# Who loads what first: moving the opening transfers between two queues, and new first orders, in a fused attention and gMLP kernel

## The chip, the cores and the metric

The kernel runs on one core of one Trainium2 chip. The metric is device microseconds for one execution, median of several runs. The engines are TensorE (PE in the profile, with its weight loads as PEld), VectorE (DVE), ScalarE (ACT), GpSimd (POOL) and SyncE (SP), which here only issues transfers. SP and ScalarE each have a queue of transfers of their own (q1 and q10 in the profile), and the transfers of both run on the same 16 DMA engines.

## The reference

The computation is a block of linear attention followed by a gMLP mixer, both with a layer norm in front and a residual behind, on x of 2048 rows by 512 columns in bfloat16:

```python
def _A_ref(x, wqkv, wo):                       # 32 heads of 16
    q, k, v = split(x @ wqkv)
    phi = lambda t: jnp.where(t > 0, t + 1, jnp.exp(t)) + 1e-06
    pq, pk = (phi(q), phi(k))
    kv = jnp.einsum('bhsd,bhse->bhde', pk, v)
    z = jnp.einsum('bhsd->bhd', pk)
    num = jnp.einsum('bhqd,bhde->bhqe', pq, kv)
    den = jnp.einsum('bhqd,bhd->bhq', pq, z)[..., None] + 1e-06
    return merge(num / den) @ wo

h  = x + _A_ref(_layernorm(x), wqkv, wo)
z  = gelu(_layernorm(h) @ w_in)                # 1792 columns, two halves of 896
g  = w_sp @ _layernorm(z[:, 896:]) + b_sp[:, None]
h2 = h + (z[:, :896] * g) @ w_out
```

Only the first step matters for the change: the layer norm of x, and the projection of its rows by the 512 columns of `wqkv` that make the keys.

## The kernel before

x is cut into 16 tiles of 128 rows. For each tile VectorE takes the statistics of the rows (`BNStats`, L576), joins them into mean and variance (the aggregate, L580), and later normalises the tile (L611) once one over the root of the variance is there. For tiles 0 to 3 ScalarE makes that root as an exponential of a logarithm (L590, L592); for later tiles GpSimd does it in pairs (L595, L597). The normalised tile must be transposed before TensorE can project it. Tiles 0 to 3 are transposed on TensorE itself, four products with the identity (L645), and ScalarE copies the result out of PSUM (L652); tiles 4 to 15 are transposed by SP's transfers (`DMA_TRANSPOSE`, L637), one after the other.

TensorE projects a tile to keys with four products of 128x512 (L734), ScalarE and VectorE turn the projections of a pair of tiles into `phi(k)` (L711, L713, L714, L717, L720), and TensorE adds up `xn^T phi(k)` over all tiles (L766). Query projections (L748) come for groups of four tiles. The later stages are the per-head products, the output projection with the residual (L904), the gMLP input (L936, L967), the mixing over rows (L1006) and the last projection (L1024).

Before there is anything to do, TensorE runs idle products on constants (L564, `keep_busy`): eight of 128x512 from the start (`WARM = 8`), two more behind the first tile's statistics, one behind its root, and four halves of 128x256 behind the transposes of tiles 0 and 1. Nobody reads their results.

Nothing is scheduled by the chip. Every operation is registered with `op(...)` in the order of the program's text and numbered; the list `ORDER` gives the order in which all of them are issued, and each engine runs its own in that order. `SLOT` gives each tile of PSUM (banks 0 to 7) and of the other pools its place. Waits are worked out from the data: an operation waits by semaphore for what it reads, and for the earlier users of its place. A wait at the head of an engine's list holds all that stands behind it on that engine. Both lists were found by a search outside this program.

The transfers at the start are registered at L510 and after. Before the change they are: on SP x tile 0, tile 2, tile 3, the query weights (512 columns of `wqkv`), tiles 4 and 5 in one transfer, then 6 and 7, 8 and 9, 10 and 11, 12 to 15; on ScalarE x tile 1 and the key weights, and behind these two the load of ScalarE's table (L555). A tile of x is 128 KB, the key weights and the query weights are 512 KB each. The value weights and what follows are loaded by GpSimd much later.

`g.first_of["act"]` is a list of operations that everything registered later on ScalarE must follow.

Of the kernel before, what the change touches and what calls it, by code (L numbers as in the profile page):

```python
# [12 lines left out]


ORDER = [
# [34 lines left out]
]  # L50
SLOT = [
# [104 lines left out]
class Program:  # L156
# [14 lines left out]
    def op(self, eng, cost, fn, r=(), w=(), bias=0.0, after=(), dma=None, nbytes=0, land=2.0, lag=None,  # L171
           mode=0):
        o = Op()
        o.eng, o.fn, o.cost, o.seq = eng, fn, cost, len(self.ops)
        o.bias, o.land, lag = bias + self.bias, land, self.LAG[eng] if lag is None else lag
        o.late, o.start, o.mode = self.late, None, mode
        o.after, o.deps, o.tiles = list(after) + self.first_of.get(eng, []), {}, []
        o.marked, o.sem, o.semval, o.grp, o.bytes, o.lag = False, None, None, dma, nbytes, lag
        o.raw = set()
        for x in list(r) + list(w):  # L180
            t = getattr(x, "tile", None)
            if t is not None and t not in o.tiles:
                o.tiles.append(t)
                t.ops.append(o)
        rk = [k for x in r for k in x.keys]
        wk = [k for x in w for k in x.keys]
        for k in rk:
            p = self.writer.get(k)
            if p is not None:
                o.deps[p] = True  # L190
                o.raw.add(p)
        for k in wk:
            p = self.writer.get(k)
            if p is not None:
                o.deps[p] = True
            for q in self.readers.get(k, ()):
                if q is not o:
                    o.deps[q] = True
        for k in rk:
            self.readers.setdefault(k, []).append(o)  # L200
        for k in wk:
            self.writer[k] = o
            self.readers[k] = []
        self.ops.append(o)
        return o
# [149 lines left out]
def bass_sequential_preLN__linear_attn_block__mixer_gmlp__prompt_kernel(  # L355
# [11 lines left out]
    _, S, D = A_x.shape  # L367
# [5 lines left out]
    TPG = GW // P  # L373
    NP = NT // 2
    assert D == 512 and KD == 4 and NG == 4 and FH == KF * P and 512 < FH <= 1024
    WARM = 8
    EPS_PHI, EPS_DEN, EPS_LN = 1e-6, 1e-6, 1e-5
    CG = 32
# [30 lines left out]
    wqkv = View(s_w3, 0, [KD, 3 * D], BF16)  # L409
# [65 lines left out]
    def bank(i):  # L475
        return lambda a: a[:, i, :]
# [4 lines left out]
    g = Program(nc)  # L481
# [12 lines left out]
    def load(eng, name, dst, src, nbytes, bias=0.0, behind=(), cost=0.5):  # L494
        o = op(eng, cost, lambda e: e.dma_start(dst.ap(), src), w=[dst], dma=(name, False), nbytes=nbytes,
               bias=bias, land=2.3)
        for p in behind:
            o.deps[p] = True
        return o

    w3 = A_wqkv.rearrange("(c p) f -> p c f", p=P)
# [3 lines left out]
    def load_x(eng, a, b, bias=BIG, **kw):  # L505
        more = {2: 40e3, 3: 60e3, 4: 70e3}.get(a, 0)
        xl[a] = load(eng, f"x{a}", x[a:b, :], x_dram[a * P:b * P, :].rearrange("(n p) d -> p n d", p=P),
                     int((b - a) * P * D * 2 + more), bias, **kw)

    load_x("sp", 0, 1)  # L510
    load_x("act", 1, 2)
    load("act", "wk", wqkv[:, D:2 * D], w3[:, :, D:2 * D], D * D * 2)
    load_x("sp", 2, 3)
    load_x("sp", 3, 4)
    load("sp", "wq", wqkv[:, 0:D], w3[:, :, 0:D], D * D * 2)
    for a in (4, 6):
        load_x("sp", a, a + 2)
    for a in (8, 10):
        load_x("sp", a, a + 2)
    load_x("sp", 12, 16)  # L520
# [39 lines left out]
    warm = []  # L560

    def keep_busy(n, cost, after, behind=()):
        row = nc.const_aps.tensor(1.0, (P, n), BF16)
        o = op("pe", cost, lambda e: e.matmul(idle(bank(0)).ap()[:, 0:n], lhsT=row[:, 0:P], rhs=row, start=True,  # L564
                                                 stop=True), w=[idle()], bias=BIG, after=after)
        for p in behind:
            o.deps[p] = True
        return o

    for i in range(WARM):  # L570
        warm = [keep_busy(512, MM, warm)]


    def stats(src, st):
# [381 lines left out]
    for tg in range(NG):  # L956
        g.bias = -GROUP * tg - 40.0
        for f0 in range(0, KF, 2):
# [18 lines left out]
         behind=[last_T[hT[0].store]])  # L977

    def load_wsp(tg, after):
        for st in range(NT):  # L980
            dst = wsp[tg][st, :]
            o = op("sp", 1.3, lambda e, dst=dst, st=st: e.dma_start_transpose(
                dst.ap(), B_w_sp[tg * GW:(tg + 1) * GW, st * P:(st + 1) * P]),
               w=[dst], dma=(f"wsp{tg}", True), nbytes=P * GW * 2, land=2.7, bias=-120.0 - 20 * tg, after=after)
            after = [o]
        return after

    bsp = Tile(BS)
    behind = [last_T[xT[0].store]]
    for tg in range(NG):  # L990
        g.late = tg > 0
        behind = load_wsp(tg, behind + ([last_T[hT[0].store]] if tg == 1 else []))
# [91 lines left out]
```

## Time and profile before

| | us |
|---|---|
| median of 3 runs | 241.08 (240.99 to 241.31) |
| the profiled execution | 241.31 |
| its span, first to last instruction | 240.1 |
| TensorE busy in the span | 235.3 |
| VectorE busy | 132.8 |
| ScalarE busy | 78.6 |
| first statistics on VectorE start | 3.50 |
| first key projection starts | 7.05 |
| third key projection starts | 9.61 |

Times in the views are microseconds from the start of the span. In a timeline row the first number is the start, the second how long, then the engine, the line of the kernel and the operation; what stands in square brackets is how long the engine was idle before and what it waited for. A queue's own instructions carry a q (SPq, ACTq). In a row of transfers the last number is the time from issue to landing. TensorE's products overlap: one is listed with its whole way through the array, so the distance from start to start is what a product costs.

### The profile page before, as it was taken

How to read it: one execution, taken by the hardware profiler on the slowest of the kernel's cores; microseconds unless marked ns; L12 is line 12 of the kernel's file. 1: busy time of each engine (PE TensorE's matmuls, PEld its weight loads, DVE VectorE, ACT ScalarE, POOL GpSimd, SP SyncE). 2: the span in 40 equal slices, each digit the busy share in tenths (PEclk: the TensorE clock that was granted, in tenths of full speed). 3: DMA queues.
4: the chain of work that ended last, by engine and by line, in shares of the span. 5: the costliest groups of instructions: out<-in, count | busy, mean ns of one | idle time of the engine just before them, and what ended most of it. 6: DMA issues, size and time to landing. Idle time of an engine off the chain costs nothing.

```text
span 240.1 us, 3026 instructions
## 1 busy us (share of the span) xinstructions
PE 235.3 (98%) x1172; PEld 110.2 (46%) x1194; DVE 132.8 (55%) x269; ACT 78.6 (33%) x101; POOL 33.3 (14%) x84
## 2 busy tenths in 40 slices
PE   7999999999999999999999999999999999999996
PEld 2544444554444444444444444444444444444443
DVE  4898884489999882938533233351332523323444
ACT  3783843884487698665400000000000000000000
POOL 7131303000334514235000000000000000000000
DMA  6930539950214463369444444445500200000022
GB/s 215 310 77 19 105 70 252 322 104 3 44 33 93 122 83 66 67 172 159 108 91 107 90 104 94 109 93 88 148 24 0 67 24 0 0 3 0 0 87 88
DMA packets 56702, 21.83 MB, mean 91 GB/s; under 512 B 50704, under 2 KB 55824, under 8 KB 56688
## 3 DMA queue, kind: packets, MB, share of 16 engines
q1 hardware_dynamic: 54928, 16.62, 33.3%
q0 software_dynamic: 944, 4.33, 5.4%
q10 hardware_dynamic: 816, 0.70, 0.9%
q8 instruction: 9, 0.15, 0.3%
q14 instruction: 5, 0.04, 0.1%
HBM read 7.47 MB, written 2.10 MB: 40 GB/s over the span
## 4 chain that ended last, share of the span: by engine, by line
PE 96%; DMA 1%; DVE 1%; issue 1%
PE ps L1006 40%; PE ps L936 10%; PE ps L1024 10%; PE ps L967 10%; PE ps L766 6%; PE ps L904 6%; PE ps L734 6%; PE ps L748 6%; DMA xh<-in_A_x_dram 1%; DVE small L576 1%; PE ps L645 1%; PE ps L858 0%; PE ps L838 0%; PE ps L782 0%; PE ps L874 0%
## 5 line engine op out<-in xcount | busy, mean ns | idle before, releaser
L1006 PE MATMUL ps<-wsp,pk_xn_z 128*128 128x512 bf16 x328 | 72.9, 379 | 0.4
L1013 DVE TENSOR_TENSOR e<-ps,e 128x512 bf16<-128x512 f32 x28 | 19.4, 692 | 66.1 <-PE ps L1006 66.1
L1006 PEld LDWEIGHTS ps<-wsp,pk_xn_z 128*128 128x128 bf16 x336 | 32.9, 98 | 39.6
L936 PE MATMUL ps<-win,hT 128*128 128x512 bf16 (+1 forms) x127 | 26.1, 352 | 0.1
L967 PE MATMUL ps<-hT,win 128*128 128x512 bf16 x108 | 25.8, 379 | 0.2
L1024 PE MATMUL ps<-wout,xT_pq_z 128*128 128x512 bf16 (+2 forms) x118 | 24.6, 366 | 0.1
L1006 PE MATMUL ps<-wqkv_wsp,pk_xn_z 128*128 128x512 bf16 x110 | 24.2, 379 | 0.1
L945 DVE BATCH_NORM_STATS2 small<-pk_xn_z 128x6 f32<-128x512 bf16 (+1 forms) x32 | 18.2, 606 | 10.6 <-ACT pk_xn_z L941 10.6
L576 DVE BATCH_NORM_STATS2 small<-xh 128x6 f32<-128x512 bf16 x32 | 21.0, 675 | 3.5 <-DMA xh<-in_A_x_dram 3.5
L711 ACT ACTIVATE e<-ps 128x1024 bf16<-128x1024 f32 x16 | 16.4, 1029 | 11.5 <-PE ps L734 8.1
L936 PEld LDWEIGHTS ps<-win,hT 128*128 128x128 bf16 x128 | 12.5, 98 | 12.7
L972 ACT ACTIVATE xT_pq_z<-ps 128x1024 bf16<-128x1024 f32 (+1 forms) x16 | 14.2, 915 | 10.0 <-PE ps L967 10.0
L1024 PEld LDWEIGHTS ps<-wout,xT_pq_z 128*128 128x128 bf16 x119 | 11.5, 98 | 13.0
L1030 DVE TENSOR_TENSOR e<-ps,xh 128x512 bf16<-128x512 f32 (+2 forms) x17 | 11.2, 660 | 11.3 <-PE ps L1024 11.3
L1006 PEld LDWEIGHTS ps<-wqkv_wsp,pk_xn_z 128*128 128x128 bf16 x112 | 11.0, 98 | 13.2
L967 PEld LDWEIGHTS ps<-hT,win 128*128 128x128 bf16 x112 | 10.9, 98 | 12.5 <-DVE xh L909 0.2
L941 ACT ACTIVATE pk_xn_z<-ps 128x896 bf16<-128x896 f32 x16 | 14.5, 918 | 4.6 <-PE ps L936 4.6
L597 POOL TENSOR_TENSOR small<-small 128x2 f32<-128x2 f32 x22 | 15.8, 720 | 1.3
L766 PE MATMUL ps<-pk_xn_z 128*128 128x512 bf16 x64 | 15.9, 379 | 0.0
L734 PE MATMUL ps<-wqkv_wsp,xT_pq_z 128*128 128x512 bf16 x63 | 15.6, 379 | 0.1
L748 PE MATMUL ps<-xT_pq_z,wqkv_wsp 128*128 128x512 bf16 x60 | 14.6, 379 | 0.3 <-issue 0.2
L904 PE MATMUL ps<-pk_xn_z,xT_pq_z 128*128 128x512 bf16 x63 | 14.2, 379 | 0.2 <-issue 0.2
(71 smaller groups left out, 173.0 us busy)
## 6 DMA issues: line engine op xcount, KB each, us to landing
out_dram<-e SPq DMA_DIRECT2D x15, 128.0 KB, 1.7
win<-in_B_w_in_dram POOLq DMA_DIRECT2D x1, 1792.0 KB, 11.3
xh<-in_A_x_dram SPq DMA_DIRECT2D x4, 256.0 KB, 6.2
wout<-in_B_w_out_dram POOLq DMA_DIRECT2D x1, 896.0 KB, 6.8
wsp<-in_B_w_sp_dram SPq DMA_TRANSPOSE x48, 2.7
wqkv_wsp<-in_A_wqkv_dram ACTq DMA_DIRECT2D x1, 512.0 KB, 4.4
wqkv_wsp<-in_A_wqkv_dram SPq DMA_DIRECT2D x1, 512.0 KB, 5.6
xh<-in_A_x_dram SPq DMA_DIRECT2D x1, 512.0 KB, 7.4
```

Source lines behind the costliest of these rows:

```text
L576: op("dve", dve_c(512), lambda e: e.bn_stats(s6.ap(), src.ap()), r=[src], w=[s6])
L711: op("act", act_c(n), lambda e: e.activation(lo.ap(), t(flat).ap(), ACT.Exp), r=[t()], w=[lo])
L734: i = e.matmul(t(bank(ti)).ap(), lhsT=lhs.ap()[:, c, :], rhs=rhs.ap()[:, c, :], start=(c == 0), stop=(c == KD - 1))
L748: r_ = e.matmul(t(bank(i)).ap(), lhsT=lhs.ap()[:, c, :], rhs=rhs.ap()[:, c, :], start=(c == 0), stop=(c == KD - 1))
L766: r = e.matmul(txk[h](bank(i)).ap(), lhsT=xx.ap()[:, c * P:(c + 1) * P], rhs=kk.ap(), start=(n == 0), stop=(n == NT - 1))
L904: i = e.matmul(t(bank(ti)).ap(), lhsT=l.ap()[:, c, :], rhs=mw[c, :].ap(), start=(c == 0), stop=(c == KD - 1))
L936: k = e.matmul(t(bank(i)).ap()[:, 0:b - a], lhsT=l.ap()[:, c, :], rhs=win[c, a:b].ap(), start=(c == 0), stop=(c == KD - 1))
L945: op("dve", dve_c(b - a), lambda e, s6=s6, src=src: e.bn_stats(s6.ap(), src.ap()), r=[src], w=[s6])
L967: k = e.matmul(t(bank(i)).ap(), lhsT=l.ap()[:, c, :], rhs=r_.ap()[:, c, :], start=(c == 0), stop=(c == KD - 1))
L1006: k = e.matmul(t(bank(0)).ap(), lhsT=l.ap()[:, s - a, :], rhs=r_.ap()[:, s - a, :], start=(s == 0), stop=(s == NT - 1))
L1013: op("dve", dve_c(512), lambda e: e.tensor_tensor(gb().ap(), t(bank(0)).ap(), bsp().ap()[:, tg * GW:(tg + 1) * GW], ALU.add), r=[t(), bsp( ...
L1024: k = e.matmul(t(bank(0)).ap()[:, 0:b - a], lhsT=l.ap()[:, fc, :], rhs=wout[fc, a:b].ap(), start=(fc == 0), stop=(fc == KF - 1))
```

## The change

The key weights stay on ScalarE, but ScalarE's table load now stands first in its list, and the weights' transfer waits for the end of the first idle product on TensorE. x tile 1 goes from ScalarE's queue to SP's, so that SP issues tiles 0, 1, 2, 3, then 4 and 5, then the query weights, then the rest. The number `GATE` says behind which idle product the weights wait.

The first part of `ORDER`, up to where the first stage ends, is replaced by another order of the same operations, and the places in PSUM of that part are dealt out anew. What this does to the first instructions of each engine:

- VectorE before: statistics 0, aggregate 0, statistics 1, aggregate 1, normalise 0, statistics 2, normalise 1, aggregate 2, statistics 3, normalise 2, aggregate 3, normalise 3, then statistics of 4 and 5. After: statistics 0 and 1, aggregates 0 and 1, statistics 2, normalise 0, aggregate 2, normalise 1 and 2, statistics 3, aggregate 3, statistics 4, normalise 3.
- ScalarE before: root 0, root 1, copy of transpose 0, root 2, copy 1, root 3, copies 2 and 3. After: roots 0, 1, 2, copies 0 and 1, root 3, copies 2 and 3.
- TensorE before: ten idle products, transposes 0, an idle product and two halves, transposes 1, key projection 0, transposes 2, key projection 1, a half, transposes 3, a half, key projections 2 and 3. After: eleven idle products, transposes 0, two halves, transposes 1, two halves, transposes 2, key projections 0 and 1, transposes 3, key projections 2 and 3. Both go on with the sixteen products of the first query projection, then six (before) or four (after) products of L766, then key projections 4 and 5.
- GpSimd: the constants are made in another order; the identity comes after the selection matrix.

All line numbers behind the new lines grow by one to three: the key projection is L734 before and L737 after. The work is the same.

```diff
 ORDER = [
-    0, 3, 4, 5, 6, 27, 1, 2, 13, 24, 14, 28, 29, 30, 31, 32, 33, 15, 21, 16, 7, 8, 34, 35, 123, 124, 11, 12, 22, 18,
...
+    0, 1, 17, 12, 23, 24, 13, 20, 10, 21, 16, 22, 11, 35, 42, 36, 43, 2, 3, 49, 26, 28, 29, 30, 31, 32, 33, 34, 25, 27,
...
 SLOT = [
-    0, 1, 1, 2, 1, 4, 0, 4, 0, 2, 1, 2, 1, 6, 1, 2, 0, 6, 0, 2, 2, 6, 0, 6, 0, 2, 6, 0, 6, 6, 2, 6, 2, 0, 6, 1, 6, 6,
...
+    0, 1, 2, 3, 3, 0, 0, 2, 0, 4, 1, 4, 1, 6, 1, 4, 0, 6, 0, 4, 0, 6, 0, 6, 2, 2, 6, 0, 6, 6, 4, 6, 4, 2, 6, 1, 6, 6,
...
+    GATE = 0
     WARM = 8
...
     load_x("sp", 0, 1)
-    load_x("act", 1, 2)
-    load("act", "wk", wqkv[:, D:2 * D], w3[:, :, D:2 * D], D * D * 2)
+    load_x("sp", 1, 2)
     load_x("sp", 2, 3)
     load_x("sp", 3, 4)
+    load_x("sp", 4, 6)
     load("sp", "wq", wqkv[:, 0:D], w3[:, :, 0:D], D * D * 2)
-    for a in (4, 6):
-        load_x("sp", a, a + 2)
+    load_x("sp", 6, 8)
     for a in (8, 10):
         load_x("sp", a, a + 2)
     load_x("sp", 12, 16)
...
     for i in range(WARM):
         warm = [keep_busy(512, MM, warm)]
+        if i == GATE:
+            load("act", "wk", wqkv[:, D:2 * D], w3[:, :, D:2 * D], D * D * 2, behind=warm)
+            g.first_of["act"].append(g.ops[-1])
```

22 rows, old and new, of tables (ORDER, SLOT) are left out of this document.

## The prediction

> **What bounds the kernel now.** First the page: busy shares and the chain that ended last.
>
> ```profile
> span 240.1 us, 3026 instructions
> PE 235.3 (98%) x1172; PEld 110.2 (46%) x1194; DVE 132.8 (55%) x269; ACT 78.6 (33%) x101; POOL 33.3 (14%) x84
> PE 96%; DMA 1%; DVE 1%; issue 1%
> ```
>
> TensorE is the bound from end to end. A reordering can only win or lose where TensorE does no useful work, so the next view is busy time by stretch.
>
> ```profile
> 0.83:5.76 4.93, 4.45 (x10) 1.17 (x11) 2.19 (x6) 2.27 (x5) 4.33 (x15) 1.00 0.75 243
> 9.61:60.00 50.39, 49.84 (x304) 24.24 (x309) 39.31 (x81) 32.44 (x39) 8.74 (x17) 1.00 0.53 125
> 60.00:230.00 170.00, 169.09 (x788) 78.38 (x803) 83.99 (x169) 41.39 (x51) 19.97 (x49) 1.00 0.34 71
> ```
>
> From 9.61 on TensorE is busy 49.84 of 50.39 us and then 169.09 of 170. In the first stretch it is busy too, but with ten idle products. The third view, the chain in order of time, shows what ends there.
>
> ```profile
> 0.79 2.68 DMA xh<-in_A_x_dram
> 3.50 0.70 DVE small L576
> ...
> 5.76 0.58 PE ps L645 x4
> ...
> 7.05 1.02 PE ps L734 x4
> ...
> 9.61 1.73 PE ps L734 x8
> 11.33 0.43 PE ps L748 x2
> ```
>
> L734 are the key projections; I call their groups of four products K0, K1, K2, ... and the transposes of x tiles 0 to 3 on TensorE T0 to T3 (L645). Before K0 the chain is the landing of x tile 0, its statistics, its normalisation, T0. By 9.61, where K2 starts, K0, K1, T0 to T3 and all fifteen idle products are done, in both kernels; what follows is the same work. **So the change is worth the shift of K2's start against 9.61**, if no new wait comes later. The profiled execution took 241.31 us (span 240.1 and 1.2 around it), 0.23 above the median 241.08; I sum against 241.31 and take 0.23 off.
>
> **The durations.** Timeline rows of the head:
>
> ```profile
> 0.79 0.40 ACTq L495 DMA_DIRECT2D xh<-in_A_x_dram  x1
> 0.79 1.33 SPq L495 DMA_DIRECT2D xh<-in_A_x_dram  x3
> 0.83 0.59 PE L564 MATMUL ps<-const-bfloat16-1.0 128*128 128x512 bf16 x1 [0.83 <-PEq L1069]
> 1.23 0.46 ACTq L495 DMA_DIRECT2D wqkv_wsp<-in_A_wqkv_dram  x1
> 1.71 1.28 ACT L555 ACT_TABLE_LOAD   x1 [1.71 <-PEq L1069]
> 4.23 0.18 DVE L580 BATCH_NORM_AGGREGATE small<-small 128x2 f32<-128x6 f32 x1
> 4.51 0.29 ACT L590 ACTIVATE small<-small 128x1 f32<-128x1 f32 x1 [1.51 <-DVE small L580]
> 4.83 0.20 ACT L592 ACTIVATE small<-small 128x1 f32<-128x1 f32 x1
> 5.12 0.50 DVE L611 TENSOR_SCALAR pk_xn_z<-xh,small 128x512 bf16<-128x512 bf16 x1
> 5.54 0.67 DVE L576 BATCH_NORM_STATS2 small<-xh 128x6 f32<-128x512 bf16 x1
> 6.14 0.39 DVE L611 TENSOR_SCALAR pk_xn_z<-xh,small 128x512 bf16<-128x512 bf16 x1
> 6.45 0.17 DVE L580 BATCH_NORM_AGGREGATE small<-small 128x2 f32<-128x6 f32 x1
> 7.20 0.20 ACT L592 ACTIVATE small<-small 128x1 f32<-128x1 f32 x1
> 7.44 0.41 DVE L611 TENSOR_SCALAR pk_xn_z<-xh,small 128x512 bf16<-128x512 bf16 x1 [0.24 <-ACT small L592]
> 7.90 0.23 PEld L645 LDWEIGHTS ps<-small,pk_xn_z 128*128 128x128 bf16 x4 [0.32 <-DVE pk_xn_z L611]
> 8.41 0.58 ACT L652 ACTIVATE xT_pq_z<-ps 128x512 bf16<-128x512 bf16 x1
> ```
>
> Start to start these give: statistics to the next instruction 0.60 (5.54 to 6.14), to their own aggregate 0.73 (3.50 to 4.23); normalisation to the next 0.31; aggregate to the next 0.10 (4.23 plus 0.10 is where the next statistics stood), to its logarithm 0.28; logarithm to exponential 0.32; exponential to normalisation 0.24; normalisation to transposes 0.46; a group of transposes 0.22; a projection 0.86 (half of 1.73); a copy 0.6.
>
> **The change, part by part.** The new first order on VectorE is statistics 0, 1, aggregates 0, 1, statistics 2, normalise 0, aggregate 2, normalise 1, 2, statistics 3, aggregate 3, statistics 4, normalise 3. On TensorE it is eleven idle products, T0, two halves, T1, two halves, T2, K0, K1, T3, K2, K3. On ScalarE the roots of tiles 0, 1, 2 come before the first two copies, the root of tile 3 before the copy of T2. T2 and T3 now share PSUM bank 3.
>
> Call t the start of statistics 2. Normalise 0 then starts at t+0.60, aggregate 2 at t+0.91, its logarithm 1.19, exponential 1.51, normalise 2 at 1.75, T2 at 2.21, K0 at 2.43; K0 and K1 end at 4.16. T3 waits for bank 3: statistics 3 at 2.06 (normalise 2 plus 0.31), aggregate 3 at 2.79, logarithm 3.07, exponential 3.39, copy of T2 3.59 to 4.19. T3 runs 4.25 to 4.47. **K2 starts at t+4.47**, against 9.61; level at t = 5.14.
>
> If nothing is late, t hangs on x tile 0: with s the start of statistics 0, aggregate 1 stands at s+1.30 and t = s+1.40, and normalise 0 waits for its root (1.20+0.28+0.32+0.29 = s+2.09, where t+0.60 is s+2.00), so K2 starts at s+5.96. With s as it is, 3.50, that is 9.46, a gain of 0.15. The idle products cost nothing: the eleventh lies beside normalise 0, the four halves wait beside normalise 1 and 2; without that cover they are 4 times 0.11 us. The table load moves from 1.71 to 0.79, worth nothing, since its first user runs at 4.51. The wait put on the key weights on ScalarE has behind it only the root of tile 0, two us later.
>
> **When the tiles land** decides the rest. Transfers by issue: x0; then key weights and x2; then x3 and the query weights; and the queues while key weights move, 3.9 to 4.8, and in the ramp, 1.8 to 2.6:
>
> ```profile
> xh<-in_A_x_dram SPq DMA_DIRECT2D x1, 128.0 KB, 2.7
> ...
> wqkv_wsp<-in_A_wqkv_dram ACTq DMA_DIRECT2D x1, 512.0 KB, 4.4
> xh<-in_A_x_dram SPq DMA_DIRECT2D x1, 128.0 KB, 2.9
> ...
> wqkv_wsp<-in_A_wqkv_dram SPq DMA_DIRECT2D x1, 512.0 KB, 5.6
> xh<-in_A_x_dram SPq DMA_DIRECT2D x1, 128.0 KB, 4.3
> ...
> DMA packets 327, 0.33 MB, mean 372 GB/s; under 512 B 0, under 2 KB 327, under 8 KB 327
> q10 hardware_dynamic: 324, 0.33, 103.7%
> q1 hardware_dynamic: 3, 0.00, 0.9%
> ...
> DMA packets 119, 0.12 MB, mean 152 GB/s; under 512 B 0, under 2 KB 119, under 8 KB 119
> ```
>
> SP's three issues in 1.33 us stand 0.44 apart: 0.79, 1.24, 1.69, and the next at 2.15. So x2 landed near 4.15, x3 near 6.0, the key weights near 5.6. Between 3.9 and 4.8 ScalarE's queue (q10) moved 324 packets and SP's (q1) three, though x3 had been issued at 1.7: once the key weights move, SP's next tile stands until they are through. x2 slipped past because x1 was ahead of the weights on their queue.
>
> Now x1 is on SP, and nothing is ahead of the weights on ScalarE's queue. The first idle product ends at 0.83+0.59 = 1.42, so they issue near 1.47, against 1.24 for x1 and 1.69 for x2, 0.24 later than before. First data came one us after the issue, so the weights stand ready near 2.5, x2 near 2.7, while x0 and x1 occupy the engines until about 3.0 (152 GB/s in the ramp). By the row above the weights then go first, and **x2 takes the place that x3 had**. x3 landed with 1 MB through, x2 lands with 128 KB less (0.35 us at 372 GB/s): 5.65; the weights themselves land 0.35 earlier too, 5.3, the lower end. I take 5.5, so t = 5.53 and K2 starts at 10.00: 0.39 late. Ends 5.3 and 5.65 give 9.80 and 10.15, a loss of 0.19 to 0.54.
>
> [...]
>
> x4 and the query weights: the weights land 256 KB later (0.7 us, near 8.5, from 2.15+5.6 = 7.8); their first product is at 11.33, so this is hidden. x4 comes earlier than before and statistics 4 waits for nothing. K0 at t+2.43 = 7.96 has its weights.
>
> Later orders: two fewer products (0.43 us) stand ahead of tile 4's projection, and tile 7's comes 1.7 us earlier against K2.
>
> ```profile
> 12.34 14.12 SPq L637 DMA_TRANSPOSE xT_pq_z<-pk_xn_z  x7
> xT_pq_z<-pk_xn_z SPq DMA_TRANSPOSE x12, 2.5
> ```
>
> Tile 4's transpose issues at 12.34 and tile 5's 1.3 later, landing near 14.8 and 16.2; tile 5 was needed near 16.9, now 0.43 earlier: 0.3 is left. I cost this at nothing; uncovered it is at most 0.1 to 0.3.
>
> Sum: 241.31 + 0.39 - 0.23 = 241.47, so **241.5**; own range 241.25 to 241.75.
>
> **Rivals.** First, x2 lands ahead of the weights, and the kernel is faster. That holds if ScalarE issues them only after its table load (0.79+1.28 = 2.07; the stated gate then does nothing), or if x2 wins on all engines. For it: the table load began at 1.71, as the issue before it ended (1.23+0.46), so these two do not overlap in that order. Against it: that is the opposite order, and nothing here shows a transfer waiting for a table load. [...] Then s also gains, since x1 no longer shares the ramp with x0: nothing at the least (3.50, a gain of 0.15), 0.4 at the most (x1's tile, 0.35 us at 372, all in front of x0). With 0.25 K2 starts at 9.21, 0.40 early: 240.7, range 240.5 to 240.95. It decides from t under 5.14, x2 landing before 5.1.
>
> Second, x1 too falls behind the weights, on engines that end x0 after 2.5. x1 then lands near 5.3, where statistics 1 want it at s+0.60, near 4; statistics 1 at 5.3, t 0.80 later at 6.1, K2 at 10.57: 242.05. Against it: x1 is issued 0.23 before the weights.
>
> Third, later waits or a slow TensorE: idle products ran at 0.43 each and projections at 0.22; with longer waits before T0 the eight products of K0 and K1 could run at the slow rate, 1.7 us more, 243. The granted clock is 1.00 in all rows, so little speaks for it.
>
> **How the numbers follow.** Forecast 0.48, first rival 0.40, second 0.08, third 0.04. About 0.2% (0.48 us) can be told from no change. Of the forecast a little over half lies beyond 241.56, with both later rivals 0.38 slower; of the first rival a little over half lies under 240.6: 0.22 faster; 0.40 between. The range, 240.5 to 242.1, leaves out the first rival's best end and the third.
>
> **What would show it.** Right: ACTq issue of the weights near 1.5, x2 landing in 5.3 to 5.65, VectorE idle before its third statistics for about a us, K2 (the second pair of L737) at 9.8 to 10.15. Wrong: the weights issued at 2.1 or x2 landed near 4, K2 near 9.2; K2 as forecast but the total elsewhere, a new wait after it; L737 pairs at 0.43 a product, the third rival.

## The result: 0.8% slower, and two groups of times

| | before | changed |
|---|---|---|
| median | 241.06 us (14 runs) | 243.47 us (14 runs) |
| lowest to highest | 240.81 to 243.0 | 241.92 to 245.42 |
| ratio, 95% interval | 1 | 1.0081, 1.0052 to 1.0111 |
| profiled execution | 241.31 us | 242.39 us |

The forecast was 241.5, range 240.5 to 242.1. The changed kernel's times fall into two groups: six from 241.92 to 242.46, and eight from 243.44 up. Six of the eight show a mean granted TensorE clock of 0.993, none of the first six does. One of the eight, at 245.42, lies more than 1 us above the others, and no profile shows why. The profiled execution is one of the first group.

One correction to what stands above: in the order before, VectorE takes the tiles as 0, 2, 1, 3 (`ORDER` issues the statistics of tile 2 second), and TensorE transposes them in that order; the list in the section on the change says 0, 1, 2, 3. The durations taken from those rows are by kind and do not depend on it, but one expectation below does.

The page after, busy shares and the chain that ended last:

```profile
span 241.2 us, 3051 instructions
PE 236.6 (98%) x1194; PEld 110.1 (46%) x1194; DVE 132.6 (55%) x269; ACT 78.6 (33%) x101; POOL 34.1 (14%) x84
PE 96%; DMA 2%; DVE 1%; SPq 0%; issue 0%
```

Nothing in these shares says where a microsecond went; DMA on the chain went from 1% to 2%. The timeline of the head does:

```profile
0.79 1.28 ACT L555 ACT_TABLE_LOAD   x1 [0.79 <-PEq L1072]
0.83 4.85 PE L564 MATMUL ps<-const-bfloat16-1.0 128*128 128x512 bf16 x11 [0.83 <-PEq L1072]
1.45 0.44 ACTq L496 DMA_DIRECT2D wqkv_wsp<-in_A_wqkv_dram  x1
2.96 1.29 DVE L579 BATCH_NORM_STATS2 small<-xh 128x6 f32<-128x512 bf16 x2 [2.96 <-DMA xh<-in_A_x_dram]
6.21 0.69 DVE L579 BATCH_NORM_STATS2 small<-xh 128x6 f32<-128x512 bf16 x1 [1.75 <-DMA xh<-in_A_x_dram]
7.37 0.38 PE L648 MATMUL ps<-small,pk_xn_z 128*128 128x128 bf16 x4 [1.68 <-DVE small L583]
```

The weights are issued at 1.45, while the table load runs. The first statistics start at 2.96 instead of 3.50, the third wait 1.75 us for x tile 2 and start at 6.21, and TensorE stands 1.68 us before T0. The transfers, by issue: the key weights with x1, then x2.

```profile
wqkv_wsp<-in_A_wqkv_dram ACTq DMA_DIRECT2D x1, 512.0 KB, 6.0
xh<-in_A_x_dram SPq DMA_DIRECT2D x1, 128.0 KB, 2.1
...
xh<-in_A_x_dram SPq DMA_DIRECT2D x1, 128.0 KB, 4.5
```

x1, issued at 1.24, took 2.1 us; x2, issued at 1.70, took 4.5 and landed near 6.2. The weights, issued at 1.45, landed at 1.45+6.0, near 7.5, so x2 was late without waiting for the end of them. While they moved, from 3.6 to 5.4, the packets of both queues (q10 is ScalarE's, q1 is SP's) were:

```profile
q10 hardware_dynamic: 394, 0.40, 69.3%
q1 hardware_dynamic: 160, 0.15, 24.0%
```

The two queues moved side by side. The chain:

```profile
1.70 4.48 DMA xh<-in_A_x_dram
...
8.77 1.73 PE ps L737 x8
10.50 0.22 PE ps L648 x4
10.72 1.73 PE ps L737 x8
```

K2 starts at 10.72 against 9.61, 1.11 late, and the span is 241.2 against 240.1. So in this execution everything is lost at x2. What the second group loses beside it, this profile cannot show.

### The profile page after: what moved, and what is told of

It is laid out like the page before. It is cut to its first block, busy times and chain, and to the rows that moved or that the text cites. A ratio compares the mean times of both kernels' runs of the same rounds, so it can differ in the third digit from the quotient of the medians.

```text
span 241.2 us, 3051 instructions
## 1 busy us (share of the span) xinstructions
PE 236.6 (98%) x1194; PEld 110.1 (46%) x1194; DVE 132.6 (55%) x269; ACT 78.6 (33%) x101; POOL 34.1 (14%) x84
## 4 chain that ended last, share of the span: by engine, by line
PE 96%; DMA 2%; DVE 1%; SPq 0%; issue 0%
PE ps L1009 40%; PE ps L939 10%; PE ps L1027 10%; PE ps L970 10%; PE ps L907 6%; PE ps L751 6%; PE ps L769 6%; PE ps L737 6%; DMA xh<-in_A_x_dram 2%; PE ps L648 0%; PE ps L861 0%; PE ps L841 0%; PE ps L785 0%; PE ps L877 0%; PE ps L822 0%; SPq L496 0%
## 5 line engine op out<-in xcount | busy, mean ns | idle before, releaser
L970 PE MATMUL ps<-hT,win 128*128 128x512 bf16 x112 | 26.3, 379 | 0.0
L751 PE MATMUL ps<-xT_pq_z,wqkv_wsp 128*128 128x512 bf16 x64 | 15.5, 380 | 0.0
L737 PE MATMUL ps<-wqkv_wsp,xT_pq_z 128*128 128x512 bf16 x64 | 15.3, 379 | 0.0
```

Of the source, the lines that this page charges most:

```text
L737: i = e.matmul(t(bank(ti)).ap(), lhsT=lhs.ap()[:, c, :], rhs=rhs.ap()[:, c, :], start=(c == 0), stop=(c == KD - 1))
L751: r_ = e.matmul(t(bank(i)).ap(), lhsT=lhs.ap()[:, c, :], rhs=rhs.ap()[:, c, :], start=(c == 0), stop=(c == KD - 1))
L970: k = e.matmul(t(bank(i)).ap(), lhsT=l.ap()[:, c, :], rhs=r_.ap()[:, c, :], start=(c == 0), stop=(c == KD - 1))
```

## The experiments

Theory 1: the key weights, issued just ahead of x2, hold it up on the DMA engines, and the new order lets everything wait for x2. Theory 2, the prediction's third rival: TensorE's long wait before T0 delays its fast rate in part of the executions. The rival to both: the new orders cost by themselves.

### The weights later: GATE = 2

```diff
-    GATE = 0
+    GATE = 2
```

> The changed kernel with GATE = 2: the key weights wait for the third idle product (ends near 2.27) and not the first; all else as changed. Theory 1 (the weights stand in front of x tile 2 on the DMA engines, and the third statistics wait for it): weights issued near 2.3, 0.6 behind x2's issue at 1.70, so x2 lands near 4, statistics 2 start at 4.4 instead of 6.21, K2 at 8.9 to 9.3 instead of 10.72, time 240.4 to 241.0, below the kernel before. Theory 2 (the long wait of TensorE before T0 delays its fast clock in part of the executions): the wait shrinks too, so the executions at 243.5 and more with a mean clock of 0.993 go. Rival (the new orders cost by themselves, whatever lands when): still 242 or more. Second risk: the weights land too late, near 7.5 or later, and K0 waits for them; then K2 is near 9.5 to 10.

Measured: median 241.68 (8 runs) beside 241.17, ratio 1.0017 (1.0005 to 1.0029); no execution at 0.993. The timeline:

```profile
2.31 0.44 ACTq L497 DMA_DIRECT2D wqkv_wsp<-in_A_wqkv_dram  x1
4.36 0.69 DVE L580 BATCH_NORM_STATS2 small<-xh 128x6 f32<-128x512 bf16 x1
7.88 1.89 PE L738 MATMUL ps<-wqkv_wsp,xT_pq_z 128*128 128x512 bf16 x8 [0.82 <-ACT small L596]
```

The transfers by issue, x2 and then the weights, and after them K2 in the chain:

```profile
xh<-in_A_x_dram SPq DMA_DIRECT2D x1, 128.0 KB, 2.6
...
wqkv_wsp<-in_A_wqkv_dram ACTq DMA_DIRECT2D x1, 512.0 KB, 5.4
```

```profile
9.99 1.73 PE ps L738 x8
```

x2 takes 2.6 us instead of 4.5, and its statistics no longer wait. Now the weights land at 2.31+5.4 = 7.7, and K0, whose transposes are done by 7.1, waits for them: the second risk named, not the gain. (The row names ScalarE as the releaser, but that exponential serves tile 3; K0 reads the weights.)

### The weights in between: GATE = 1, measured twice

The same edit with 1.

> The changed kernel with GATE = 1: the weights issue near 1.87, 0.17 behind x2's issue (1.70) instead of 0.25 ahead of it (1.45). Theory 1: x2 goes first on most or all DMA engines and lands near 4.3, so statistics 2 start near 4.4; the weights land earlier than the 7.74 they had with GATE = 2, near 7.2, K0 near 7.3 and K2 near 9.4, 240.8 to 241.3. If some engines still take the weights first, x2 lands at 5 or later in part of the executions, and the times spread between 241 and 242.5. Theory 2: no wait of TensorE over a us before T0, so no mean clock of 0.993.

Measured: median 240.98 (12 runs, 240.75 to 241.55) beside 241.24, ratio 0.9987 (0.9977 to 0.9996). The timeline, x2 among the transfers, and K2 in the chain:

```profile
1.88 0.44 ACTq L497 DMA_DIRECT2D wqkv_wsp<-in_A_wqkv_dram  x1
4.78 0.69 DVE L580 BATCH_NORM_STATS2 small<-xh 128x6 f32<-128x512 bf16 x1 [0.40 <-DMA xh<-in_A_x_dram]
```

```profile
xh<-in_A_x_dram SPq DMA_DIRECT2D x1, 128.0 KB, 3.1
```

```profile
9.29 1.73 PE ps L738 x8
```

Three issues of the weights against the same issue of x2 at 1.70: 0.25 ahead of it x2 took 4.5 us (4.1 to 4.5 in the four profiles with that issue), 0.18 behind it 3.1 (2.9 in the run below), 0.61 behind it 2.6. That is theory 1 in one row of numbers.

> GATE = 1 once more, to see whether its small gain over the kernel before (ratio 0.9987) stands. Theory 1: x2 lands under 5.1 again, K2 near 9.3, 240.7 to 241.2, ratio 0.997 to 0.9995. If the gain was chance: 0.9995 to 1.001.

Measured: 241.13 (12 runs) beside 241.10, ratio 0.9994 (0.9983 to 1.0005). K0 started here at 7.38, against 7.17 in the first profile, and K2 at 9.49, against 9.29. So this version undoes the loss; it has the orders of the changed kernel, which therefore cost nothing with these landings. A gain of 0.1% over the kernel before is possible and not settled.

### TensorE kept busy: five idle products instead of one

```diff
-    def keep_busy(n, cost, after, behind=()):
+    def keep_busy(n, cost, after, behind=(), reps=1):
...
+        def mm(e):
+            for _ in range(reps):
+                i = e.matmul(idle(bank(0)).ap()[:, 0:n], lhsT=row[:, 0:P], rhs=row, start=True, stop=True)
+            return i
+        o = op("pe", cost * reps, mm, w=[idle()], bias=BIG, after=after)
...
-            keep_busy(n, cost, [], [gate] if gate.eng != "pe" else [])
+            keep_busy(n, cost, [], [gate] if gate.eng != "pe" else [], reps=5 if gate is rs_op[0] else 1)
```

> The changed kernel, with five idle products of 128x512 instead of one behind the root of tile 0: TensorE is kept busy from 5.0 to about 7.2, where it stood still 1.7 us before T0. Theory 2: no execution shows a mean clock of 0.993, none is above 242.6, the median is 242.0 to 242.4 (the landing of x2 is as late as before). If the wait of TensorE is not what delays the fast clock: about half of the executions stay at 243.4 to 245, median about 243.5.

Measured: median 242.16 (6 runs, 241.79 to 242.92) beside 241.17, ratio 1.0044 (1.0031 to 1.0057); no execution at 0.993. The timeline, and K2 in the chain:

```profile
0.83 5.72 PE L567 MATMUL ps<-const-bfloat16-1.0 128*128 128x512 bf16 x15 [0.83 <-PEq L1076]
6.05 0.69 DVE L583 BATCH_NORM_STATS2 small<-xh 128x6 f32<-128x512 bf16 x1 [1.64 <-DMA xh<-in_A_x_dram]
7.20 0.38 PE L652 MATMUL ps<-small,pk_xn_z 128*128 128x128 bf16 x4 [0.65 <-DVE small L587]
```

```profile
10.56 1.73 PE ps L741 x8
```

x2 is nearly as late as before and K2 at 10.56; TensorE stands 0.65 us before T0 instead of 1.68, and the second group of times is gone: none of the six executions took over 242.92, where 12 of the 22 unchanged ones (14 above, 8 below) took 243.4 or more. Four products whose results nobody reads make the kernel faster: 0.44% is left where the unchanged version lost 0.81%, and 0.72% when it was measured again (below). The intervals of these ratios touch, so the size of the gain is rough.

### The changed kernel again

> The changed kernel unchanged, on the chip and beside the runs of GATE = 1. Theories 1 and 2 together: x2 lands near 6.1, K2 at t+4.5 near 10.6 where TensorE is fast in time (241.9 to 242.6), and 1.2 to 1.8 later in about half of the executions, whose first key products stand 0.43 apart; median 242.5 to 243.7. If the spread of the first measurement belonged to that chip: all at 242.

Measured: median 242.88 (8 runs, 241.59 to 245.05) beside 241.10, ratio 1.0072 (1.0037 to 1.0107). This profile caught an execution of the second group, 243.4 us. The timeline, and then the chain:

```profile
5.86 0.69 DVE L579 BATCH_NORM_STATS2 small<-xh 128x6 f32<-128x512 bf16 x1 [1.33 <-DMA xh<-in_A_x_dram]
7.02 0.58 PE L648 MATMUL ps<-small,pk_xn_z 128*128 128x128 bf16 x4 [1.33 <-DVE small L583]
```

```profile
8.46 0.43 PE ps L564 x2
8.88 0.43 PE ps L648 x4
9.31 2.22 PE ps L737 x8
11.53 0.22 PE ps L648 x4
11.76 1.29 PE ps L737 x6
```

x2 came earlier than in the first profile, so K2 should start at 5.86+4.51 = 10.37. It starts at 11.76. Groups of transposes take 0.43 instead of 0.22, and K0 and K1 take 2.22 instead of 1.73: TensorE runs at half rate until after 9.31, where the other execution had transposes at the full rate from 7.37. That is the 1.4 us of the second group. The mean clock of this execution is listed as 1.00, so the mean does not find all of them; the distance of the products does.

### The other side: the kernel before with less idle work

```diff
-        warm = [keep_busy(512, MM, warm)]
+        warm = [keep_busy(512 if i < 6 else 128, MM if i < 6 else MM / 4, warm)]
...
-    for gate, n, cost, count in ((first[0], 512, MM, 2), (rs_op[0], 512, MM, 1), (tr_op[0], 256, MM / 2, 2),
+    for gate, n, cost, count in ((first[0], 128, MM / 4, 2), (rs_op[0], 128, MM / 4, 1), (tr_op[0], 256, MM / 2, 2),
```

> The kernel before with less idle work on TensorE: the last two of the eight first idle products, the two behind the first statistics and the one behind the first root are 128 columns instead of 512, so TensorE stands still some 1.9 of the us between 3.4 and 5.76 instead of 0.5. Nothing else waits for these products. Theory 2 (the clock is granted by how busy a stretch of TensorE was): part of the executions show a mean clock of 0.993 and 242.5 to 243, the rest stay at 241.1. If idle work has nothing to do with it: all at 241.0 to 241.3.

Measured: median 242.48 (12 runs, 240.81 to 243.98) beside 241.24, ratio 1.0048 (1.0026 to 1.007); three executions at 0.993, two as fast as the kernel before. The chain:

```profile
7.25 1.71 PE ps L734 x4
8.96 0.43 PE ps L645 x4
9.39 0.99 PE ps L734 x4
...
10.82 1.73 PE ps L734 x8
```

K0 stands at 7.25, 0.2 behind the kernel before, but its four products take 1.71, where four at 0.22 are 0.86, and K2 starts at 10.82 instead of 9.61. Five shortened idle products cost 1.2 us here. With the fill this shows theory 2 from both sides. The products go from 0.43 apart to 0.22 near 6.3 in the profile of the kernel before and near 9.5 in this one. What sets that moment in a single execution, so that one kernel with one wait falls into two groups, no run shows.

### One part alone

The new orders with the transfers of before (`ORDER` and `SLOT` of the changed kernel in the kernel before, renumbered):

> The new orders and PSUM places with the transfers of the kernel before (x1 and the key weights on ScalarE's queue ahead of its table load, no wait on an idle product; query weights ahead of tiles 4 and 5). Theory 1: x2 lands near 4.15, statistics 2 start at 4.9, K2 at 9.46, time 240.9 to 241.1, no different from before. Rival (the orders themselves cost): 242 or more.

Measured: 242.56 (4 runs) beside 241.17, ratio 1.0054 (1.0039 to 1.0069). My expectation was wrong. The timeline, x4 among the transfers, and K2 in the chain:

```profile
7.43 1.89 PE L735 MATMUL ps<-wqkv_wsp,xT_pq_z 128*128 128x512 bf16 x8
9.57 0.69 DVE L577 BATCH_NORM_STATS2 small<-xh 128x6 f32<-128x512 bf16 x1 [1.62 <-DMA xh<-in_A_x_dram]
10.18 0.40 DVE L612 TENSOR_SCALAR pk_xn_z<-xh,small 128x512 bf16<-128x512 bf16 x1
```

```profile
xh<-in_A_x_dram SPq DMA_DIRECT2D x1, 256.0 KB, 6.9
```

```profile
11.11 1.73 PE ps L735 x8
```

x2 was in time and K0 started at 7.43. But in the new order the statistics of tile 4 stand ahead of the normalisation of tile 3, and with the query weights issued ahead of tiles 4 and 5 that transfer landed at 2.65+6.9 = 9.55: T3 and K2 waited. So these orders cost 1.4 us with those transfers, and need tile 4 early, which the change's transfers give them.

The new transfers with the orders of before:

> The new transfers with the orders and PSUM places of before. Theory 1: x2 lands at 5.5 to 6.2 here too, but now only the normalisation of tile 1 and T1 stand behind its statistics, T0 is done by then; K0 near 7.5, K2 near 9.9, about 0.3 behind the kernel before, 241.3 to 241.9. Theory 2: a wait of TensorE of a us or more before T1, so some executions at 243 and more. If the new transfers cost nothing by themselves: 240.6 to 241.1.

Measured: 243.8 (4 runs) beside 241.17, ratio 1.0106 (1.0083 to 1.0128), two executions at 0.993. The loss is larger than expected: the order before takes tile 2 second (the correction above), so everything but the first statistics waits for x2. The timeline, and K0 in the chain:

```profile
5.78 0.69 DVE L580 BATCH_NORM_STATS2 small<-xh 128x6 f32<-128x512 bf16 x1 [1.96 <-DMA xh<-in_A_x_dram]
7.14 0.59 PE L649 MATMUL ps<-small,pk_xn_z 128*128 128x128 bf16 x4 [1.88 <-DVE pk_xn_z L615]
```

```profile
9.01 1.55 PE ps L738 x4
```

x2 lands late here too (5.76), TensorE stands 1.88 us, and K0 takes 1.55, where four products at 0.22 are 0.86: both theories again, with other orders.

### All in one queue

```diff
     load_x("sp", 2, 3)
+    load("sp", "wk", wqkv[:, D:2 * D], w3[:, :, D:2 * D], D * D * 2)
     load_x("sp", 3, 4)
...
-        if i == GATE:
-            load("act", "wk", wqkv[:, D:2 * D], w3[:, :, D:2 * D], D * D * 2, behind=warm)
-            g.first_of["act"].append(g.ops[-1])
```

> The new orders, but the key weights go on SP's queue between x2 and x3, with no wait on an idle product, and ScalarE issues nothing at the start. Theory 1 (the loss is the sharing of the DMA engines between two queues): in one queue the tiles land in their order, x2 near 3.9, weights near 5.5, x3 near 6, x4 near 6.7; statistics 2 at 4.36 or a little after, T2 done near 6.9, K0 near 7, K2 at 8.9 to 9.1, 240.3 to 240.7: faster than the kernel before by 0.4 to 0.8. Rival (the orders cost, or one queue alone is too slow): K2 at 9.6 or later, 241 or more. Theory 2: no execution at 0.993.

Measured: 241.48 (12 runs) beside 241.24, ratio 1.0011 (0.9998 to 1.0023). A miss. The profiled execution, 241.99, is one of the slower of the twelve. Its timeline, and K2 in the chain:

```profile
4.39 0.66 DVE L578 BATCH_NORM_STATS2 small<-xh 128x6 f32<-128x512 bf16 x1
7.56 1.89 PE L736 MATMUL ps<-wqkv_wsp,xT_pq_z 128*128 128x512 bf16 x8 [0.32 <-DMA wqkv_wsp<-in_A_wqkv_dram]
7.78 0.69 DVE L578 BATCH_NORM_STATS2 small<-xh 128x6 f32<-128x512 bf16 x1 [1.00 <-DMA xh<-in_A_x_dram]
```

```profile
10.27 1.73 PE ps L736 x8
```

x2 came in time, as theory 1 has it. But the weights landed near 7.5, and x3 at 7.75 behind the same 1 MB of transfers that had brought it in by 6.0 in the kernel before. By 6.0 the DMA engines had moved 1.02 MB here and 1.29 MB there; why one queue is 1.7 us slower stays open.

## Why the prediction was wrong, step by step

**Right: where the loss arises.** The weights issued at 1.45 (1.47 forecast), not after the table load, x2 came late, and VectorE waited 1.75 us for it before its third statistics.

**Right: K2 from the third statistics.** The forecast was t+4.47. Measured: 6.21 to 10.72 in the changed kernel, 4.78 to 9.29 with GATE = 1, 6.05 to 10.56 with the fill: t+4.51 three times. The bank that T3 was to wait for cost nothing: T3 follows K1 at once (8.77+1.73 = 10.50). With GATE = 2 and in the single queue the weights or x3 came later, so the formula did not apply.

**Wrong: how x2 comes to be late, and so when it lands.** The step "the weights then go first, and x2 takes the place that x3 had", with the weights at 5.3 and x2 at 5.5, failed. x2 landed at 6.2, 6.0, 5.8 and 5.8 in the four profiles of these transfers, and in the first of them the weights landed at 7.5, after it. SP's queue did not stand until they were through, as it had for x3 in the kernel before (3 packets of 327): it moved 160 of 554 packets beside them. Nor did the engines move as much as the step took over from that kernel. From 2.7 to 4.5, first in the kernel before and then in the changed one:

```profile
DMA packets 605, 0.57 MB, mean 317 GB/s; under 512 B 48, under 2 KB 605, under 8 KB 605
DMA packets 348, 0.33 MB, mean 186 GB/s; under 512 B 21, under 2 KB 348, under 8 KB 348
```

The 0.24 MB that are missing are 0.6 us at 372 GB/s, about what x2 is later than forecast in this profile; 0.39 late became 1.11. The slow stretch alone does not hold up x2: with GATE = 2 the engines moved 0.36 MB in the same time, and x2, whose packets went first there, landed by 4.3. So the 0.7 us more go to the sharing and the slow stretch together, as these counts have it; no run varied the rate of the engines, and why they are slow there stays open.

**Wrong: the third rival.** "The granted clock is 1.00 in all rows, so little speaks for it", chance 0.04. It came true in about half of the executions, at 1.4 us against the 1.7 it was priced at, and makes a little under half of the loss in the median: with TensorE kept busy 0.44% is left of 0.81% and 0.72%. The rows to read were quoted: idle products 0.43 apart, projections 0.22, so a switch lay near 6 us in the kernel before, and the forecast itself put T0 0.8 us later, with one idle product more in front of it and the rest a wait. The mean clock, listed as 1.00 there, does not show it.

**First rival, half right.** s did move, from 3.50 to 2.96, more than the 0.4 allowed: x0, with x1 behind it on its own queue, lands 2.1 us after its issue instead of 2.7. With GATE = 1, where x2 does go first, this is nearly all spent on x2, which took 3.1 and 2.9 us beside the weights, and in the second profile on K0, which started at 7.38: the kernel comes out level or 0.1% ahead, not at 240.7.

**Second rival.** x1 did not fall behind the weights: it landed 2.1 us after its issue, near 3.3.

## What to carry to other kernels

A large transfer on another queue, issued a quarter of a microsecond ahead of a small urgent one, held it up for 1.5 to 1.9 us here; issued just behind it, for 0.3 to 0.5 (both against the 2.6 us that it took with GATE = 2). When transfers and orders are searched together, test the order against the landings measured with those transfers: here each half alone, with the other half as before, lost to the kernel before (0.5% and 1.1%), and so did both together until the weights were issued 0.43 us later. Before a wait is moved to the start of a kernel, look at the distance from product to product on TensorE: in one of the two profiles of the changed kernel a wait of 1.33 us before T0 was followed by products at half rate until after 9.31, which cost 1.4 us more.

## What the hardware showed that was not expected

- Four idle products more made the changed kernel faster (242.16 against medians of 243.47 and 242.88), and five shortened ones made the kernel before slower by 0.5%.
- The same kernel gave K0 and K1 together in 1.73 or 2.22 us in its two profiles, the slower time in the execution whose x2 came earlier, and an execution at half rate up to about 9 to 10 us still lists a mean clock of 1.00.
- From 3.2 to 3.5 us in the changed kernel, about where the weights begin, the 16 DMA engines moved 41 GB/s. It does not take a second queue: with all in one queue they moved 58 GB/s from 3.6 to 3.9, and with GATE = 2 126 GB/s from 2.7 to 3.3, before the first packet of the weights. What makes this slow stretch was not found.
